# Which weights are asked for first, and a new order for the whole program: linear attention followed by a gated mixer on one core

## The chip, the cores and the metric

The kernel runs on one core of one Trainium2 chip. The metric is device time in microseconds (us) for one launch, the median of several runs.

## The reference, cut to what matters

For each of 8 batches there are 8 heads of 576 tokens with 64 features. Everything is float32 in memory.

```python
kv  = einsum('bhsd,bhse->bhde', k, v)
out = einsum('bhsd,bhde->bhse', q, kv)
x   = out / sqrt(mean(out*out, -1) + 1e-6) * g_norm      # then (batch, 576, 512)
theta  = x @ w_theta                                      # 512 x 512
zr, zi = x * cos(theta), x * sin(theta)
y = einsum('ts,bsd->btd', w_tok_r, zr) + einsum('ts,bsd->btd', w_tok_i, zi)   # 576 x 576 each
u = x + y
return u + relu(u @ w_ch)                                 # 512 x 512
```

## The kernel before

One batch has 576 tokens: four tiles of 128 tokens (j = 0 to 3) and a tail of 64. The tail is packed so that it fills 128 partitions at half width, and what concerns it has an "e" in its name. Each batch passes through the same chain of tasks:

- `kv` (L244, 80 fp32 rows of the trace for each batch) multiplies keys by values into PSUM. `ko` (L260) copies the result to the block-diagonal `kbd`.
- `qt` and `qo` (L279, L287) turn the queries on TensorE for batches 0 to 2; later batches use a transposing DMA on SP's queue (`qd`, L294). `raw` (L305) is query times kbd.
- `sq` (ScalarE, L330), `ss` (VectorE, L340) and `rt` (GpSimd, L346; for batch 0 ScalarE and VectorE) make one over the root of the head's mean square. `x` (VectorE, L368) scales by it.
- `xt` and `xc` (L391, L412) turn x on TensorE and copy it out, times g, to `xT`; from batch 4 on a DMA does the turning (`xd`, `xo`).
- `th` (L448) is x times theta's weights `wth`. `pt`, `ar`, `ab`, `si`, `co` (L453 to L487) bring the angle into range, take its absolute value and give sine and cosine. `z` (L493) multiplies them by x.
- `y` (L522) mixes the tokens, in three parts of three matmuls each for every one of 8 output pieces, with the turned token weights `wT`. `um` (L537) makes u.
- `ut`, `uo` (L544, L557) or, for batches 3 to 6, the DMA `ud` turn u back. `v` (L568) is u times the channel weights, `fin` (L573) adds and clips, `st` (L609) stores.

The token weights come in two halves, `w_tok_r` and `w_tok_i`. Each is turned on TensorE once, in nine pieces (`wt`, L622): even pieces and the tail need the i half and its 64 tail rows, odd pieces and the tail the r half.

All of these are 1189 tasks in a list. Each task has an engine, or two between which one is chosen, and the tasks whose results it needs. The table `TURNS` (L32) says in which order they are issued: a plain number is a task on its first engine, a number with a star is the same task on its second engine, and `r9` or `a5` are so many idle matmuls on TensorE, which keep it running and compute nothing that is used. `play` (L86) issues them in that order. Nothing is moved afterwards, so each engine and each DMA queue meets its instructions in the order of the table.

The loads around the change stand on three queues. SP carries batch 0's keys and tails and then all later keys and values; ACT carries batch 0's values; POOL (GpSimd) carries the queries and all weights, since these change from float32 to float16 on the way. Three small GpSimd instructions hold transfers back on purpose. `hold p` (L231) reads one number of batch 0's v tails and so waits until they have landed; whatever comes behind it on POOL's queue waits too. `hold w` (L228) reads a number of theta's weights, and batch 1's v (`load v1`, on SP, with batch 1's k behind it) waits for it. `hold v` waits for batch 1's v and stands ahead of the queries of batches 1 and 2 and the channel weights `wch`.

Of the kernel before, what the change touches and what calls it, by code (L numbers as in the profile page):

```python
# [33 lines left out]
58* 31 32 36 37 38 33* 34 39* 40* 73 43 74* 50* 44 45 59 75 51 65 25 60 12 61 76 46 66 77 47 62 63  # L34
52 r9 48 64 67 53 68 84 82 85 99 54 78 83* 69 70 100 135 139 136 140 79 80 71 55 56 72 92 90 91* 93
86 87* 127 88 101 89* 94 106 120 81 103 102 128* 95 131 137 113 132* 96 138* 104 121 122 105 129 97
114 107 130* 98 108 115 109 143 133 124 123* 134 169 173 141 161 210 211 212 213 110 125 111 144 117
116* 118 142 126 112 119 174 162 216 217* 214 215 170 230 163 223 218 219 231* 165 175 232 171 164
354 203 205 204 206 220 172 176 388 233 221 234 389 166 145 157 167 153 237 224 374 146 154 222 168
225 238* 235 226 236 155 156 227 147 149 244 239 158 375 245 240 251 150 151 187 159 252 241 228 242  # L40
261 253 262 188* 152 148 160 229 381 189 263 243 246 254 382 194 367 255 268 190 368* 256* 177 178*
275 257 182 247 265 264* 266 269 248 249 361 362 363 364 276 270 277 278 267 258* 250 183 279 271*
282 184 259 272 273 283 192 365* 366* 369 383 284 185 260 289 197 199 370 358 209 208 359 360 509
356 357 355 191 529 518 512 513 514 515 371 372 384 193 290 198 274 291 385 195 280 285* 373 281 200
386 292* 293 286 516 294 179 376 387 324 312 404 390 325 377 517 196 540 505 506 507 508 287 180 405
378 316 317 313 402 391 295 288 419 395 314 318 326 392 379 393 380 403 420 396 315 319 327 394 304
397 300 398 399 412 421 400 413 414 519 305 520 401 521 522 408 406 407 320 306 307 296 530 410 531
416 415 422* 423 424 417 411 301 409* 532 533 297 321 302 303 523 308 309 322 323 310 524 525 311
418 534 298 426 427 343 433 548 434 299 428 526 541 542 543 440 441 442 443* 435 544 186 511 527 430
429* 652 653 654 655 658 669 645 646 647 181* 510 425 549* 431 444 656 437 657 344* 545 345 546 554  # L50
563 436 432 555* 346 547* 528 564 445 565 348 584 349 535 536 438 328 556 338 467 468 475 659 585
557 446 439 537 586 339 469 470 558 476 477 455 340 451 452 588 660 329 661 649 785 651 538 650 539
787 662 341 456 670 453 454 560 559* 567 587* 671 672 663 561 457 550 447 552 471 472 458 553 478
673 674 347 680 648 686 473 474 675 333 335 334 336 794 337 805 783 330 676 677 331 577 664 463 589
566* 551 578 568 562 448 449 450 579 464 465 459 665 570 666 678 667 580* 581 571 569 572 466 582
460 461 574 687 668 573* 575 462 679 788 789 790 791 350 681 499 501 351 583 500 682 792 793 502 590
576 688 784 683 684 201* 921 479 699 700 692 693 694 795 489 490 591 685 701 332 503* 342 202 816
781 690 796 797 798 703 611 612 592 494 607 613 614 608 593 594 609 491 806 689* 713 702* 696 807
695* 697 492 808 610 595 619 620 621 481 495 484 596 597 698 799 809 714 715 810 623 782 822 493 930
704 480 482 800 598 622 599 600 811 706 801 802 707 812 705 708 710 709* 691* 615 616 603 604 605  # L60
813 485* 606 803 804 496 617 618 601 486 716* 717 602 786 814 639 817 720 641 487 818 640 819 497
642 924 925 926 927 820 815 821 823 721 722 723 711 718 712 719 928 929* 835 836 483 626 624 625 498
488 824 633 630 634 837 931 828 631 724 932 725 726 747 627 748 755 838* 628 749 936 750 756 727 829
937 938 830 933 743 744 745 757 758 746 735 728 729 730 636 632* 952 917 352* 826 941 919 918 939
934 504* 644* 825 849 751 637 739 740 940 741 947 832 839 831* 833 850 834 759 752 753 851 935 948
949 731 942 736 732 733 950 638* 754 742 842 737 853 840 852* 943 827 843 734 944 777 856 775 854
776 857 920 635 629 1059 951 738 953 760 762 761 945 1053 1054 1055 1056 844 841 946 858 845* 954
846 859* 955 855 778 847 860 956 957 848 1057 861 1058 922 958 1070 862 769 772 763 1060 863 864 770
773 1061 1062 865 959* 866 879 880 881 766 1065 1066 764 882 867 868 964 971 1063 1064 1071 1067 923
771 774* 960 962 1068 767 965 966 869 887 883 884 888 972 973 1069 885 871 1072 1073 765 643 353 895  # L70
1081 768* 1074 779* 974 870 886 967* 975 968 963 976 977 889 890 1075 872 992 1076 875 873 876 961
1077 993 874 994 877 891 892 893 969 996 995* 997 1078 878 978 979 894 970 985 980 986 982 981* 911
1082 913 912* 987 988* 983 914 998 984 908 899 905 1015 1016 989 990 896 780 897 898 1087 900 901
1079 991 999 1000 1017 1001 906 1018 1080 902 1011 1012 1013 903 1002 1083 1088 909 1014 1084 1093
1094 1095 1100 1101 1007 1008 1009 1019 1023 1102 1027 1028 1029 1024 1089 1085 916 1031 904 1086
1096* 1090 1097 1104 907 1091 910 1030 1103* 1025 1003 1004 1005 1020 1021 1010 1026 1006 1107 1022
1105 1098 1092 1106 1099 1108 1114 1115 1109 1121 1110 1047 1034 1033 1049 1048 1050 1116 1038 1041
1111 1122 1123 1112 1113 1124* 1125 1118 1126 1117* 1119 1032 1039 1040 1042 1043* 1156 1035 1036
1144 1157 1148 1149 1145 1152 1153 1127 1120 1146 1150 1154 1158 1151 1147 1155 1159 1037 1044 1136
1132 1045 1180 1178 1137 1138 1139 1179 1181 1133 1128 1183 1185 1173 1140 1141 1134 1184 1186 1129  # L80
1130 1135 1182 1188 1187 1131 1142 1143 1175 1160 1162 1046* 1174* 1176 1161* 1177 915* 1165 1163
1164 1051* 1167 1170 1052* 1166 1168 1171 1169 1172
""".split()


# [14 lines left out]
def kernel(  # L100
# [61 lines left out]
    wth = const.tile([P, NKC, C], FP16, name="wth")  # L162
# [17 lines left out]
    def tails_of(t):  # L180
        return t[:, H * NJ * D:H * NT * D].rearrange("p (h e) -> p h e", h=H)
# [29 lines left out]
    def token_in(w_in, at):  # L211
        nc.gpsimd.dma_start(
            out=wn[at][:], in_=w_in[0:SM, :].rearrange("(p j) s -> p j s", j=NJ)
        )

    def token_tail_in(w_in, at):
        nc.gpsimd.dma_start(out=wnt[at][:], in_=w_in[SM:S, :])
# [13 lines left out]
    def hold_pool(src):  # L231
        nc.gpsimd.tensor_copy(out=gate[:], in_=src)
# [422 lines left out]
    got, q_got, k_got = {}, {}, {}  # L655
# [9 lines left out]
    for hp in range(NHP):  # L665
# [265 lines left out]
```

## Time and profile before

| what | value |
|---|---|
| time, three runs | 207.13, 207.51 and 210.13 us; the median is 207.51 |
| the profiled execution | 206.56 us, of which the instructions span 204.6 |
| granted TensorE clock | 1.0 in every stretch |
| moved by DMA | 43.14 MB; 33.06 read, 9.44 written in HBM |

The profile is that of one execution. Busy times count an engine's own work; the time of a matmul includes its way through the array, so several overlap. "L534" is a line of the kernel. In a list of instructions the first column is the start, the second the time taken, both in us; the brackets at the end tell how long the engine was idle before it and what ended that. In the table of stretches "(x52)" is a number of instructions. In the DMA rows q0 is POOL's queue, q1 SP's and q10 ACT's.

### The profile page before, as it was taken

What the parts mean: (1) busy time and instruction counts of PE and PEld (TensorE: products, weight loads), DVE (VectorE), ACT (ScalarE), POOL (GpSimd) and SP (SyncE); (2) the same over time, 40 slices, a digit from 0 to 9 for tenths busy, and PEclk for the clock granted to TensorE, in tenths of its full rate; (3) what the DMA queues carried; (4) which work ended last, traced back from release to release, by engine and by line L of the source; (5) the groups of instructions that cost most, each with busy time, mean ns of one, the idle gap of its engine ahead of it and who ended that gap; (6) DMA issues with size and microseconds to landing.
All of it is one profiled execution on the core that took longest, in us unless ns stands there. A gap on an engine that the chain in (4) does not pass through costs nothing.

```text
span 204.6 us, 5267 instructions
## 1 busy us (share of the span) xinstructions
PE 188.3 (92%) x2078; PEld 132.8 (65%) x2078; DVE 172.5 (84%) x362; ACT 137.6 (67%) x272; POOL 86.4 (42%) x92
## 2 busy tenths in 40 slices
PE   0299899999999999999999999998989999999992
PEld 0275568885786777676776767665856746755671
DVE  6029896789999999999898999897989999689473
ACT  2006899748799587987896769576945983976101
POOL 8022061263965564874609382283629430101210
PEclk9999999999999999999999999999999999999999
DMA  6999999999999999999999999799988652853154
GB/s 196 271 197 193 294 268 193 275 354 236 254 187 193 277 264 260 310 221 137 199 226 248 237 221 180 170 283 305 287 187 194 150 103 70 189 129 135 35 154 154
DMA packets 74951, 43.14 MB, mean 211 GB/s; under 512 B 44576, under 2 KB 71008, under 8 KB 74928
## 3 DMA queue, kind: packets, MB, share of 16 engines
q1 hardware_dynamic: 58688, 32.12, 66.9%
q0 software_dynamic: 15040, 9.52, 29.9%
q10 hardware_dynamic: 1200, 1.18, 1.7%
q8 instruction: 16, 0.26, 0.5%
q14 instruction: 7, 0.06, 0.1%
HBM read 33.06 MB, written 9.44 MB: 208 GB/s over the span
## 4 chain that ended last, share of the span: by engine, by line
PE 67%; ACT 12%; DVE 8%; DMA 7%; issue 2%; POOL 1%; DVEq 0%; ACTq 0%; POOLq 0%
PE y L534 29%; PE th L440 11%; PE v L440 11%; DMA vt<-in_v_dram 5%; PE kv L255 3%; PE raw L312 3%; DMA uD<-wn 2%; DVE arg L463 2%; ACT kbd L275 2%; ACT sc L488 2%; PE wps L630 2%; ACT sc L481 1%; ACT arg L471 1%; ACT xT L408 1%; PE qps L270 1%
## 5 line engine op out<-in xcount | busy, mean ns | idle before, releaser
L353 POOL TENSOR_TENSOR rt<-ss,mhalf 128x8 f32<-128x8 f32 (+1 forms) x35 | 54.6, 1563 | 65.7 <-DVE ss L343 65.5
L534 PE MATMUL y<-wT,zm 128*128 128x320 f16 (+1 forms) x512 | 76.8, 286 | 0.7 <-DVE ot L576 0.5
L534 PEld LDWEIGHTS <-zm 128*128 128x128 f16 x512 | 48.0, 98 | 15.8 <-issue 1.2
L539 DVE SCALAR_TENSOR_TENSOR wn<-y,gcol,xT 128x320 f16<-128x320 f32 (+1 forms) x64 | 31.0, 511 | 6.7 <-PE y L534 6.3
L440 PE MATMUL th<-wth,xT 128*128 128x512 f16 x128 | 32.1, 380 | 0.9 <-ACT xT L408 0.6
L456 ACT ACTIVATE arg<-th 128x512 int32<-128x512 f32 (+1 forms) x40 | 21.8, 554 | 14.1 <-PE th L440 13.7
L440 PE MATMUL v<-wch,wn 128*128 128x512 f16 x124 | 30.7, 380 | 0.0
L255 PE MATMUL kv<-vt,kt 128*64 128x64 f32 x640 | 21.9, 230 | 9.3 <-DMA vt<-in_v_dram 9.3
L334 ACT ACTIVATE sqb<-raw 128x512 f32<-128x512 f32 x32 | 18.9, 595 | 14.4 <-PE raw L312 14.3
L255 PEld LDWEIGHTS kv<-vt,kt 128*64 128x64 f32 x640 | 20.9, 144 | 10.2 <-issue 9.7
L488 ACT ACTIVATE sc<-arg,quarter 128x512 f16<-128x512 f32 (+1 forms) x40 | 26.6, 675 | 0.3
L463 DVE SCALAR_TENSOR_TENSOR arg<-th,arg 128x512 f32<-128x512 f32 (+1 forms) x40 | 25.0, 632 | 1.9 <-ACT arg L456 1.5
L481 ACT ACTIVATE sc<-arg 128x512 f16<-128x512 f32 (+1 forms) x40 | 22.7, 582 | 3.2 <-DVE arg L463 2.8
L343 DVE TENSOR_REDUCE ss<-sqb 128x8 f32<-128x520 f32 x32 | 22.0, 687 | 2.4 <-ACT sqb L334 2.4
L511 DVE TENSOR_TENSOR zm<-x,sc 128x1024 f16<-128x1024 f16 x32 | 21.8, 686 | 1.8 <-ACT sc L488 1.5
L375 DVE TENSOR_TENSOR x<-raw,rt 128x512 f16<-128x512 f32 x32 | 21.8, 685 | 0.8 <-POOL rt L353 0.5
L440 PEld LDWEIGHTS <-xT 128*128 128x128 f16 x128 | 11.6, 98 | 11.1 <-ACT xT L408 1.0
L440 PEld LDWEIGHTS <-wn 128*128 128x128 f16 x124 | 11.5, 98 | 10.7 <-issue 0.4
L471 ACT ACTIVATE arg<-arg 128x512 f32<-128x512 f32 (+1 forms) x31 | 17.5, 575 | 1.2 <-DVE arg L463 1.1
L534 PE MATMUL y<-wT,zt 128*128 128x320 f16 (+1 forms) x64 | 18.3, 286 | 0.0
L275 ACT CAST kbd<-kv 64x256 f16<-64x256 f32 (+1 forms) x24 | 8.5, 356 | 13.5 <-PE kv L255 13.2
L275 ACT COPY us<-ups 128x512 f16<-128x512 f16 (+1 forms) x17 | 8.5, 498 | 12.6 <-PE ups L270 11.5
(83 smaller groups left out, 229.3 us busy)
## 6 DMA issues: line engine op xcount, KB each, us to landing
vt<-in_v_dram SPq DMA_DIRECT2D x7, 1024.0 KB, 9.8
kt<-in_k_dram SPq DMA_DIRECT2D x7, 1024.0 KB, 7.9
out_dram<-ot SPq DMA_DIRECT2D x24, 256.0 KB, 2.8
qh<-in_q_dram POOLq DMA_DIRECT2D x7, 512.0 KB, 8.6
out_dram<-ot POOLq DMA_DIRECT2D x7, 256.0 KB, 4.0
kt<-in_k_dram SPq DMA_DIRECT2D x2, 512.0 KB, 4.6
vt<-in_v_dram ACTq DMA_DIRECT2D x2, 512.0 KB, 9.0
kt<-in_k_dram SPq DMA_DIRECT2D x8, 128.0 KB, 7.9
```

The source lines that it names most:

```text
L255: nc.tensor.matmul(t[i * D:(i + 1) * D, hp - lo, :], ks, vs, start=(hp == lo and j == 0), stop=(hp == lo + n - 1 and j == NT - 1),)
L343: nc.vector.reduce_sum(out=ss[:], in_=sq_sb.pop((b, j))[:], axis=AXX)
L353: nc.gpsimd.tensor_tensor(out=rt[:], in0=ss[:], in1=mhalf[:, 0:h], op=ALU.pow)
L375: nc.vector.tensor_tensor(out=x_pair[b, p][:, :, a * HC:(a + 1) * HC].rearrange("p t (h e) -> p h t e", e=D), in0=r[:].rearrange("p (h t e ...
L440: nc.tensor.matmul(t[:], piece(kc), w[:, kc, :], start=first, stop=last)
L456: nc.scalar.activation(out=arg[:, 1, :].bitcast(I32), in_=th_ps[b, j][:], func=AFT.Copy, scale=1.0 / TURN)
L463: nc.vector.scalar_tensor_tensor(out=arg[:, 0, :], in0=th_ps.pop((b, j))[:], scalar=1.0 / TURN, in1=arg[:, 1, :].bitcast(I32), op0=ALU.mul ...
L481: nc.scalar.activation(out=sc[:, 0, :], in_=arg_sb[b, j][:, 0, :], func=AFT.Sin, bias=0.0, scale=TURN * SHRINK,)
L488: nc.scalar.activation(out=sc_sb[b, j][:, 1, :], in_=arg_sb.pop((b, j))[:, 1, :], func=AFT.Sin, bias=quarter[:], scale=-TURN * SHRINK,)
L511: nc.vector.tensor_tensor(out=dst, in0=x.unsqueeze(1).broadcast_to((P, 2, w)), in1=sc[:], op=ALU.mult)
L534: nc.tensor.matmul(t[:, 0:hi - lo], s, wT[:, w, lo:hi], start=n == 0, stop=n == len(z) - 1)
L539: nc.vector.scalar_tensor_tensor(out=uTb[b % NUT][:, c, lo:hi], in0=y_ps.pop((b, h, c))[:, 0:hi - lo], scalar=gcol[:, 0:1], in1=xTb[b % NX ...
```

## The change

The weights of theta and the i half of the token weights change places at `hold p`: the main part of the i half (`load toki`) is issued ahead of it, and theta's weights (`load wth`) depend on it now. The r half depends on it as before. The tail rows of the i half (`load tokie`) lose the dependence on `hold p`, but the new table issues them behind `load wth`. Batch 1's v still waits for theta's weights, through `hold w`.

`TURNS` is new throughout. The same 1189 tasks are issued in another order, other copies and absolute values have the star, and there are 7 idle matmuls (`a1`, `a1`, `a5`) where there were 10 (`r1`, `r9`).

```diff
 TURNS = """
-3 4 0 1 2 5 6 7 9 8 11 10 13 29 30 41 r1 49 35 14 15 16 17 18 19 22 23 20 21 24 26 207 28 27 42* 57
...
+0 1 6 7 8 3 4 41 9 13 a1 49 42* 50 5 11 2 10 29 30 31 32 15 16 14 17 18 19 22 24 26 27 207 28 25 20
...
-    got["wth"] = [add("load wth", "POOL", theta_in)]
+    got["tok", 0] = [add("load toki", "POOL", lambda: token_in(moe_w_tok_i, 1)),
+                     add("load tokie", "POOL", lambda: token_tail_in(moe_w_tok_i, 1))]
     hold = add("hold p", "POOL", lambda: hold_pool(tails_of(vt[0])[0:1, 0, 0:1]), [v0[2]])
-    got["tok", 0] = [add("load toki", "POOL", lambda: token_in(moe_w_tok_i, 1), [hold]),
-                     add("load tokie", "POOL", lambda: token_tail_in(moe_w_tok_i, 1), [hold])]
+    got["wth"] = [add("load wth", "POOL", theta_in, [hold])]
     got["tok", 1] = [add("load tokr", "POOL", lambda: token_in(moe_w_tok_r, 0), [hold]),
                      add("load tokre", "POOL", lambda: token_tail_in(moe_w_tok_r, 0), [hold])]
```

The first place is the start of POOL's queue, as the difference shows it. `wn` and `wnt` are the token weights and their tail rows, `gate<-vt_66` is `hold p`.

```order
 L206 DMA qe_71<-in_q_dram 64x4x64 x2
+L212 DMA wn_86<-in_moe_w_tok_i_dram 128x2304
+L232 COPY gate<-vt_66 1x1
 L220 DMA wth<-in_moe_w_theta_dram 128x4x512
-L232 COPY gate<-vt_66 1x1
-L212 DMA wn_86<-in_moe_w_tok_i_dram 128x2304
 L217 DMA wnt_88<-in_moe_w_tok_i_dram 64x576
 L212 DMA wn_85<-in_moe_w_tok_r_dram 128x2304
```

The i half's main part now stands ahead of the gate and theta's weights behind it; the i half's tail rows come behind theta's weights, and the r half is where it was.

The second place is the start of SP's queue. `kt_64` and `vt_66` are batch 0's keys and values, the 64x8x64 rows their tails; `vt_67` and `kt_65` are batch 1's.

```order
 L184 DMA kt_64<-in_k_dram 128x4x256 x2
+L190 DMA vt_66<-in_v_dram 64x8x64
+L226 DMA gcol<-in_g_norm_dram 64x1
 L190 DMA kt_64<-in_k_dram 64x8x64
-L190 DMA vt_66<-in_v_dram 64x8x64
-L226 DMA gcol<-in_g_norm_dram 64x1 x2
+L226 DMA gcol<-in_g_norm_dram 64x1
 L184 DMA vt_67<-in_v_dram 128x8x256
-L190 DMA vt_67<-in_v_dram 64x8x64
 L184 DMA kt_65<-in_k_dram 128x8x256
 L190 DMA kt_65<-in_k_dram 64x8x64
+L190 DMA vt_67<-in_v_dram 64x8x64
```

Batch 0's v tails, which `hold p` waits for, are asked for ahead of its k tails, and batch 1's v tails come last of its four loads instead of second.

The third place is ScalarE's queue around the sines of batch 1, before the change:

```order
L481 ACTIVATE sc<-arg 128x512
L471 ACTIVATE arg<-arg 128x512
L488 ACTIVATE sc<-arg,quarter 128x512
L456 ACTIVATE arg<-th 128x512 x2
L275 COPY us<-ups 128x512
L481 ACTIVATE sc<-arg 128x512
L471 ACTIVATE arg<-arg 128x512
```

and the same place in the changed kernel:

```order
L481 ACTIVATE sc<-arg 128x512
L456 ACTIVATE arg<-th 128x512
L488 ACTIVATE sc<-arg,quarter 128x512
L408 ACTIVATE xT_83<-xps,gcol 128x4x128
L456 ACTIVATE arg<-th 128x512
L481 ACTIVATE sc<-arg 128x512
L488 ACTIVATE sc<-arg,quarter 128x512
```

The absolute values (L471) of these tiles are gone from ScalarE; they stand on VectorE now (L473), as does the copy of u. Over the whole program these moves go from ScalarE to VectorE: 8 absolute values of full tiles and 2 of tails, 2 copies of u and 3 of its tails, 3 tails of `xT` and 1 piece of the token weights. From VectorE to ScalarE go 2 copies of turned queries, 1 copy of kbd and 2 of batch 0's, 1 of `xT` and 1 of its tails. Of the stores, 25 are on POOL's queue where there were 16.

More of the change, by code (lines that the diff above doesn't have):

```diff
@@ L79 @@
[L79 to L82, printed above, removed]
+0 1 6 7 8 3 4 41 9 13 a1 49 42* 50 5 11 2 10 29 30 31 32 15 16 14 17 18 19 22 24 26 27 207 28 25 20
+21 23 35 36 37 38 39* 33 34 43 44 40 73 57 58* 59 65 45 46 74* 47 60 75 61 76 66 62 a1 a5 51 52 48
@@ new lines @@
+375 235 168 222 225 226 236 227 237 381 145 238 146 147 382* 239 240 251 158 159 187 228 148 241
+188* 160 189 190 242 252 253 244 245 261 254 192 151 262 229 243 246 268 193 156 247 263 248 249 255
+256 367 194 368* 152 257 275 182 361 362 363 364 264 195 265 269 270 250 271 266 267 183* 258 276
+277 272 278 259 282 184 273 365 260 366* 369 383 283 279 370 274 185 289 197 199 384 280 290 371
+198* 284 286 285* 287 200 385 281 291 293 512 513 514 515 358 209 208 509 359 510 372 505 529 518
+386 360 373 288 387 179 177 376 312 324 292* 294 178 180 377 516 404 405* 313 395 325 517 390 378
@@ new lines @@
+1107 1106 1092* 1099 1108 1114 1121 1047 1049 1115 1109 1110 1048 1050 1116 1111 1122 1112 1123 1033
+1113 1032 1041 1038 1035 1156 1157 1042 1036 1039 1117* 1118 1125 1124* 1119 1126 1120 901 916*
+1043* 1040* 1037 1052 503* 1051 1148 1144 1149 1145 1152 1153 1127 1158 1159 1154 1155 1150 1146
+1132 1147 1151 1044 1045 1183 1185 1184 1186 1128 1178 1180 1179* 1181 1140 1133 1141 1134 1135 1173
+1129 1142 1130 1136 1143 1137 1131 1138 1139 1175 1174* 1176 1160 1162 1161* 1163 1177 1164 1165
+1167 1188* 1046* 1182* 504* 1187* 1166* 1168 1169 1170 1171 1172
```

81 lines of the change are left out of this document (36 added, 45 removed).

## The prediction

> **What bounds the kernel now.** I read the totals and the chain that ended last first, then the table of stretches, then the start instruction by instruction.
>
> ```profile
> span 204.6 us, 5267 instructions
> PE 188.3 (92%) x2078; PEld 132.8 (65%) x2078; DVE 172.5 (84%) x362; ACT 137.6 (67%) x272; POOL 86.4 (42%) x92
> PE 67%; ACT 12%; DVE 8%; DMA 7%; issue 2%; POOL 1%; DVEq 0%; ACTq 0%; POOLq 0%
> ```
>
> TensorE (PE) holds two thirds of the chain, and VectorE (DVE) is busy almost as long as PE. Which of them limits depends on the stretch. I cut the span where PE begins, where the key-value product (kv) of batch 1 begins (32.8), where that of batch 7 begins (144.7), and look at one inner stretch by itself. Columns: length, then busy time of PE, weight loads, DVE, ScalarE (ACT) and GpSimd (POOL), clock, DMA share, GB/s.
>
> ```profile
> 9.10:32.80 23.70, 22.25 (x235) 14.86 (x235) 18.08 (x46) 14.63 (x33) 6.50 (x12) 1.00 1.19 235
> 32.80:144.70 111.90, 110.32 (x1359) 81.02 (x1359) 102.31 (x205) 88.03 (x173) 59.84 (x52) 1.00 1.16 240
> 52.00:107.00 55.00, 54.31 (x738) 40.08 (x737) 52.27 (x106) 47.12 (x97) 32.75 (x29) 1.00 1.18 229
> 144.70:201.00 56.30, 55.72 (x498) 36.88 (x492) 48.06 (x98) 33.42 (x65) 15.61 (x17) 1.00 0.62 143
> ```
>
> Between 32.8 and 144.7 DVE works 102.31 of 111.9 us (91.4%), and from 52 to 107 it works 52.27 of 55 (95.0%). That is the highest share it holds for long. PE shows as busy throughout, but busy is not full pace, so I priced its work by its densest pieces on the chain (start, length, what):
>
> ```profile
> 32.86 2.48 PE kv L255 x80
> ...
> 70.53 0.45 PE xps L270 x8
> ...
> 163.70 1.73 PE th L440 x8
> ...
> 165.79 0.44 PE v L443 x8
> ...
> 174.84 5.63 PE y L534 x45
> ```
>
> A y matmul is 5.63/45 = 0.125 us, a full theta or channel matmul 1.73/8 = 0.216, a tail one 0.055, a kv row 0.031, a 128-wide turn or raw 0.056. With the counts: 576 x 0.125 = 72; 252 x 0.216 = 54.5; 128 x 0.055 = 7; 640 x 0.031 = 20; 318 x 0.056 = 18; the narrow ones, the token weights' turns and 10 idle matmuls about 10.5. Together 182 us. Ahead of batch 1's kv stand 17.7 of them, in 23.7 us, so 6.0 are lost at the start. Behind it stand 164.3, and from 32.8 to 201 are 168.2, so only some 4 us are lost there, 2.4 of them before 144.7. **PE therefore leaves little to gain after 32.8 us; DVE is close behind it in the middle; the start has the largest loss.**
>
> The start, from the timeline:
>
> ```profile
> 4.38 0.80 POOL L220 DMA_DIRECT2D wth<-in_moe_w_theta_dram  x1
> ...
> 13.93 0.17 POOL L232 COPY gate<-vt 1x1 f32<-1x1 f32 x1 [8.74 <-DMA vt<-in_v_dram]
> 14.05 0.55 POOL L212 DMA_DIRECT2D wn<-in_moe_w_tok_i_dram  x1
> ...
> 17.02 0.18 POOL L229 TENSOR_TENSOR gate<-vt,wth 1x1 f32<-1x1 f32 x1 [0.78 <-DVE qT L277]
> 17.22 0.37 SPq L184 DMA_DIRECT2D vt<-in_v_dram  x1
> ...
> 17.79 2.11 PE L640 MATMUL idle<-fill,ident 128*128 128x512 f16 x9
> ...
> 19.90 5.71 SPq L190 DMA_DIRECT2D kt<-in_k_dram  x1
> ...
> 20.80 0.68 ACT L408 ACTIVATE xT<-xps,gcol 128x512 f16<-128x512 f16 x1
> ...
> 21.53 1.04 PE L440 MATMUL th<-wth,xT 128*128 128x512 f16 x4 [0.60 <-ACT xT L408]
> ```
>
> The first theta matmul (21.53) waits for xT, not for its weights. Those had landed by 17.02, when `hold w` ran and let batch 1's v go (17.22). The idle matmuls at 17.79 fill a hole; the last thing before theta is batch 0's own chain raw, squares, root, x, xT.
>
> **The change part by part.** *Theta behind `hold p`.* What each queue moved, from the DMA view of 14.5 to 17, of 17 to 21 and of 24.4 to 27, and the times to landing:
>
> ```profile
> q0 software_dynamic: 311, 0.47, 118.1%
> ```
>
> ```profile
> q0 software_dynamic: 251, 0.79, 103.9%
> q1 hardware_dynamic: 1, 0.00, 0.1%
> ```
>
> ```profile
> q1 hardware_dynamic: 1209, 0.81, 113.7%
> ```
>
> ```profile
> wn<-in_moe_w_tok_i_dram POOLq DMA_DIRECT2D x1, 576.0 KB, 6.5
> wn<-in_moe_w_tok_r_dram POOLq DMA_DIRECT2D x1, 576.0 KB, 8.5
> wth<-in_moe_w_theta_dram POOLq DMA_DIRECT2D x1, 512.0 KB, 12.5
> ```
>
> POOL's queue (q0) alone fills the engines from 14.5 to 21, at 0.47/2.5 to 0.79/4 = 0.19 to 0.20 MB a us. Before, theta landed at 4.38 + 12.5 = 16.9 and the i half at 14.05 + 6.5 = 20.5. Swapped, the i half, 0.06 MB more, lands at about 17.2, and theta 0.5/0.2 = 2.6 us later, at 19.8. It is issued when `hold p` lets go, at 13.9 or earlier (v's tails now stand second on SP), so it queues behind the i half in any case, and how early the gate opens is worth nothing. Theta at 19.8 is 1.7 us ahead of 21.5: the first theta matmul does not feel it. The i half at 17.2 is 3.3 us earlier, so one turn of it now fits ahead of the second x turn and theta, where PE waited. That turn also reads the i half's tail rows, which stand behind theta: about 20.2, just in time. I take 0.3 us of gain here.
>
> *Batch 1's v behind theta.* It goes out at about 20.1, 2.9 later. Behind it on SP's queue are batch 1's k, k tails and v tails, and kv of batch 1 waits for all four. But v, issued at 17.22, moved one packet before 21, because the engines were full of weights. With v later the weights have them alone and end earlier. v and k (2.3 MB) then run at 0.81/2.6 = 0.31 MB a us, 7.4 us from about 23.6, to 31. Before, the last of them landed at 19.90 + 11.3 = 31.2:
>
> ```profile
> kt<-in_k_dram SPq DMA_DIRECT2D x1, 128.0 KB, 11.3
> ```
>
> Batch 1's kv begins at 32.86, so this is hidden with 1.7 us to spare, and I cost it at nothing. Without that cover the 2.9 us delay costs 2.9 - 1.7 = 1.2; that is the upper end of the start, and -1.5 (a quarter of the 6.0 lost there) the lower. *Fewer idle matmuls*, 3 x 0.216 = 0.65, stand in the hole and belong to those 1.5.
>
> One rule of the Trainium skill speaks against the swap ("DMA: Bandwidth & Descriptors", section on queues, rings and completion order): each DMA engine takes turns between the queues that have work, packet by packet, so a load issued early gets its share beside another queue. By that rule v would lose its turn for 2.9 us, at most 1.5 us of full rate, which is inside the 1.7 us to spare. The trace agrees only from 21 on; from 17.22 to 21 v has one packet beside 251 of q0.
>
> *The new order from batch 1 on.* PE does the same work there. DVE and ACT do not: a count of the two tables gives the moves, and these rows their prices (count, then busy, mean ns):
>
> ```profile
> L471 ACT ACTIVATE arg<-arg 128x512 f32<-128x512 f32 x24 | 14.7, 621 | 0.6 <-DVE arg L463 0.6
> L473 DVE TENSOR_SCALAR arg<-arg 128x512 int32<-128x512 int32 x8 | 3.6, 452 | 0.1
> L277 DVE COPY us<-ups 128x512 f16<-128x512 f16 x6 | 2.5, 419 | 0.5 <-PE ups L270 0.5
> L277 DVE COPY us<-ups 128x256 f16<-128x256 f16 x1 | 0.3, 281 | 0.0
> L277 DVE COPY qT<-qps 128x512 f16<-128x512 f16 x7 | 3.0, 422 | 9.4 <-PE qps L270 9.4
> L277 DVE CAST kbd<-kv 64x256 f16<-64x256 f32 x6 | 2.5, 420 | 0.1
> L277 DVE CAST kbd<-kv 64x128 f16<-64x128 f32 x6 | 1.7, 288 | 0.2
> L410 DVE TENSOR_SCALAR xT<-xps,gcol 128x512 f16<-128x512 f16 x8 | 3.8, 478 | 0.0
> L275 ACT COPY us<-ups 128x512 f16<-128x512 f16 x10 | 5.9, 587 | 11.5 <-PE ups L270 11.5
> ```
>
> To DVE come 8 x 0.452 (absolute values), 2 x 0.29 (their tails, priced like the 0.281 copy), 2 x 0.419 + 6 x 0.281 (u, its tails, xT's tails) and one weight piece of about 0.45: 7.2 us. Away go 2 x 0.422, 2 x 0.420, 4 x 0.288, 0.478 and about 0.35: 3.7. DVE gains 3.5 us of durations, and ACT loses about 6, 8 x 0.621 being most of it.
>
> Adding mean durations in table order between batch 1's and batch 7's kv gives DVE 114.0 us in the old table and 119.8 in the new, because the new one also places DVE work earlier. The old 114.0 showed as 102.31 busy (neighbours overlap), a factor of 0.897; the new ones come to 107.5 us. To fit in 111.9 DVE would have to run at 96.1%. At its best long share, 95.0%, the stretch takes 113.2: +1.3. At its old share, 91.4%, it takes 117.6: +5.7. The best that PE allows is its 2.4 us of loss: -2.4. I take +1.3, since ACT, relieved by about 4 us in the same stretch (101.3 to 97.2 counted likewise), should make DVE wait less than before.
>
> *The end.* Behind 144.7 PE has the same tasks in both tables, and DVE about 1 us less. The last copy of u, 0.587 us on ACT before, is one of 0.419 on DVE: -0.2, with bounds of -1.5 (PE's loss there) and +0.5 (a store on POOL that ends last).
>
> **Sum:** -0.3 + 1.3 - 0.2 = +0.8 on the profiled execution's 206.56, its span of 204.6 and 2 us around it, so 207.4. The median shown is 207.51, 0.95 above the profiled one, which makes the forecast **208.3 us**: no change that can be told, since about 2% (4 us) is what this kernel's measurement can tell.
>
> **The rivals.** *DVE becomes the bound.* It keeps its old share of waits between 32.8 and 144.7, so its 5.2 us of added busy time push batch 7's kv by 5.7: 206.56 - 0.3 + 5.7 - 0.2 + 0.95 = 212.7, slower. It decides from batch 2's kv on, at the absolute values. For it: DVE's 95% from 52 to 107 hold there already. Against it: ACT, with 12% of the chain, has less to do. Chance 0.2. A rule of the skill sharpens it ("SBUF — State Buffer", section on the shared port): DVE in its two-port modes and GpSimd lock each other out, and the absolute values and copies are candidates for such modes. The roots on GpSimd show a spread that would fit:
>
> ```profile
> L353 POOL TENSOR_TENSOR rt<-ss,mhalf x35: 1006/1642/1959, 39.4 to 174.7; 128x8 f32<-128x8 f32 x28, 128x4 f32<-128x4 f32 x7
> ```
>
> No run here shows which instruction stretched them.
>
> *ACT was the brake.* Its chain pieces shrink, DVE runs above 95%, and PE gets back all it loses: -2.4 in the middle, -0.8 at the start, -0.2 at the end, 206.56 - 3.4 + 0.95 = 204.1; with the whole of the bounds (-1.5 - 2.4 - 1.5) 202.1. For it: 12% of the chain on ACT. Against it: DVE has to reach 96%. Chance 0.25.
>
> *Batch 1's kv waits for its loads.* v's first packet comes as long after its issue as before and the weights are no faster: k lands at 34.1, kv of batch 1 begins 1.2 later, and the rest follows: 208.3 + 0.3 + 1.2 = 209.8. Chance 0.1. Here the change would not do what it says on the one side that can lose: the swap brings only a wait, and the order carries the rest.
>
> **How the numbers follow.** My forecast, a result between 206.5 and 210, has 0.45, DVE 0.2, ACT 0.25, the loads 0.1. The range of 204.0 to 213.0 holds the forecast, the loads, the centre of the DVE case and that of the ACT case; 0.2 stay outside, most of it in the ACT case's lower half. Faster by over 2% (below 203.4) is 0.17, a good half of the ACT case and a little of the start's bound; slower by over 2% (above 211.7) 0.22, the DVE case and the two mishaps that add to it; 0.61 for within 2%.
>
> **What would show it.** Right: theta lands at 19 to 20.5 and its first matmul begins within 0.5 us of 21.5; batch 1's v is issued near 20 and its kv begins within 1 us of 32.8; batch 7's kv begins 0 to 3 us after 144.7 with DVE at 94 to 96% between them; PE's stretch behind it stays at 56 us. Wrong: PE waiting for theta's weights or the i half's tail rows, kv of batch 1 waiting for a load, DVE below 92% with PE idle on it, or batch 7's kv ahead of 143.

## The result, and the profile after

| | before | after |
|---|---|---|
| median of 20 runs each (us) | 207.12 | 210.75 |
| lowest and highest (us) | 206.04, 210.13 | 208.41, 212.96 |
| the profiled execution (us) | 206.56 | 208.41 |

The change costs time: the ratio is 1.015, with a 95% interval of 1.012 to 1.018. It leaves out runs that lie over 1.5% above the fastest of the same kernel; where a kernel's runs spread widely, its median over all runs is given beside it. The forecast was 208.3, so the time came out 2.45 above it, inside the range of 204 to 213 and inside the 2% that I had called "no change". The profiled execution of the changed kernel is the lowest of its 20 runs, so its trace shows the least of the loss.

The totals of the changed kernel, then its stretches, cut at the same events as before (PE begins, kv of batch 1 begins, kv of batch 7 begins), with the one between batch 5's and batch 6's kv besides:

```profile
span 206.6 us, 5255 instructions
PE 187.0 (91%) x2075; PEld 133.3 (65%) x2075; DVE 173.7 (84%) x371; ACT 132.9 (64%) x263; POOL 90.9 (44%) x101
```

```profile
10.70:33.41 22.71, 21.11 (x230) 15.06 (x230) 16.22 (x40) 16.43 (x38) 6.71 (x12) 1.00 1.21 234
33.41:147.25 113.84, 110.48 (x1358) 81.08 (x1359) 103.83 (x214) 83.20 (x165) 62.14 (x55) 1.00 1.22 240
100.83:126.14 25.31, 22.69 (x273) 16.49 (x274) 21.05 (x44) 17.87 (x35) 12.69 (x13) 1.00 1.23 229
147.25:203.00 55.75, 55.44 (x492) 37.14 (x488) 49.48 (x104) 31.80 (x61) 17.80 (x23) 1.00 0.55 134
```

The stretch between batch 5's and batch 6's kv, in the kernel before:

```profile
100.72:123.35 22.63, 22.51 (x274) 16.45 (x274) 21.27 (x43) 17.79 (x36) 11.81 (x10) 1.00 1.14 223
```

The spans differ by 2.0 us. Batch 1's kv begins 0.6 late (33.41 against 32.8). By batch 5's kv this is nearly regained (100.83 against 100.72). Then one stretch takes 25.31 us where it took 22.63: 2.7 us lost in one place, with the same PE work, 22.69 busy against 22.51. Behind batch 7's kv nothing is lost. So the loss is a hole, not a general slowing. **The hole**, from the timeline of the changed kernel:

```profile
85.55 1.01 SPq L184 DMA_DIRECT2D vt<-in_v_dram  x1
...
94.08 2.02 SPq L298 DMA_TRANSPOSE qD<-qh  x1
...
96.19 0.62 SPq L190 DMA_DIRECT2D vt<-in_v_dram  x1
...
97.30 4.96 SPq L421 DMA_TRANSPOSE xD<-x  x1
...
108.06 1.15 ACT L408 ACTIVATE xT<-xD,gcol 128x1024 f16<-128x1024 f16 x1 [2.81 <-DMA xD<-x]
...
109.27 1.04 PE L440 MATMUL th<-wth,xT 128*128 128x512 f16 x4 [2.50 <-ACT xT L408]
```

and what the DMA view says of the transpose issued at 97.30 (count, then us from issue to landing):

```profile
xD<-x SPq DMA_TRANSPOSE x1, 10.7
```

Batch 4's x is turned by a DMA on SP's queue (`xd 4 0`). It stands there behind the 1 MB of batch 6's values (85.55), a turn of batch 5's queries (94.08) and the 128 KB of batch 6's value tails (96.19), and takes 10.7 us to land. ScalarE stands idle for 2.81 us on it, and since it meets its instructions in the order of the table, all that it would do next waits too; PE then waits 2.50 for the `xT` that ScalarE makes. Before, the same transpose was ahead of that load:

```profile
95.27 1.25 SPq L421 DMA_TRANSPOSE xD<-x  x1
...
99.97 0.57 SPq L184 DMA_DIRECT2D vt<-in_v_dram  x1
...
102.22 1.13 ACT L408 ACTIVATE xT<-xD,gcol 128x1024 f16<-128x1024 f16 x1
```

```profile
xD<-x SPq DMA_TRANSPOSE x1, 3.2
```

It landed in 3.2 us, 3.7 before ScalarE came to it. The Trainium skill says of such queues ("DMA: Bandwidth & Descriptors", section on queues, rings and completion order) that on each DMA engine the descriptors of one ring are consumed in ring order; the trace agrees: by the DMA view the four take 14.5, 10.5, 8.9 and 10.7 us, so they land at 100.1, 104.6, 105.1 and 108.0, in the order in which they were issued, and the transpose behind the bulk takes three times as long as before.

**The start** of the changed kernel, from the timeline:

```profile
11.60 0.75 POOL L220 DMA_DIRECT2D wth<-in_moe_w_theta_dram  x1
...
12.09 4.54 PE L255 MATMUL kv<-vt,kt 128*64 128x64 f32 x80
...
16.56 0.40 PE L312 MATMUL raw<-kbd,qT 128*128 128x128 f16 x4
...
19.26 0.18 POOL L229 TENSOR_TENSOR gate<-vt,wth 1x1 f32<-1x1 f32 x1 [5.27 <-DMA wth<-in_moe_w_theta_dram]
19.47 0.39 SPq L184 DMA_DIRECT2D vt<-in_v_dram  x1
...
22.08 0.69 ACT L408 ACTIVATE xT<-xps,gcol 128x512 f16<-128x512 f16 x1
...
23.04 1.03 PE L440 MATMUL th<-wth,xT 128*128 128x512 f16 x4
```

Theta's weights are there at 19.26, but the first theta matmul begins at 23.04, 1.5 later than before. It isn't the weights: the chain ahead of it is late from batch 0's kv on. PE now begins with a turn of queries, at 10.70, where it began with kv at 9.11. Batch 0's kv stands behind that turn as one block of 80 rows that takes 4.54 us, 57 ns a row. Before, its last 32 rows took 36 ns each, and the first raw began 0.86 earlier:

```profile
14.21 1.15 PE L255 MATMUL kv<-vt,kt 128*64 128x64 f32 x32
...
15.70 1.30 PE L312 MATMUL raw<-kbd,qT 128*128 128x128 f16 x8
```

From the first raw to batch 1's kv the changed kernel takes 16.85 us (16.56 to 33.41), and the kernel before 17.09 (15.70 to 32.79). So the start loses all that it loses ahead of the first raw.

### The profile page after: what moved, and what is told of

It reads as the page before. It is cut to its first block, busy times and chain, and to the rows that moved or that the text cites. A ratio compares the mean times of both kernels' runs of the same rounds, so it can differ in the third digit from the quotient of the medians.

```text
span 206.6 us, 5255 instructions
## 1 busy us (share of the span) xinstructions
PE 187.0 (91%) x2075; PEld 133.3 (65%) x2075; DVE 173.7 (84%) x371; ACT 132.9 (64%) x263; POOL 90.9 (44%) x101
## 5 line engine op out<-in xcount | busy, mean ns | idle before, releaser
L534 PE MATMUL y<-wT,zm 128*128 128x256 f16 (+1 forms) x512 | 76.7, 286 | 0.2
L539 DVE SCALAR_TENSOR_TENSOR wn<-y,gcol,xT 128x256 f16<-128x256 f32 (+1 forms) x64 | 31.5, 512 | 3.9 <-PE y L534 3.7
L334 ACT ACTIVATE sqb<-raw 128x512 f32<-128x512 f32 x32 | 18.4, 597 | 13.1 <-PE raw L312 13.0
L255 PEld LDWEIGHTS kv<-vt,kt 128*64 128x64 f32 x640 | 21.5, 149 | 0.8 <-issue 0.5
L440 PEld LDWEIGHTS <-xT 128*128 128x128 f16 x128 | 11.5, 98 | 12.1 <-ACT xT L408 2.7
L534 PE MATMUL y<-wT,zt 128*128 128x256 f16 (+1 forms) x64 | 18.3, 286 | 0.0
L270 PE MATMUL qps<-ident,qh 128*128 128x128 f16 x48 | 4.8, 234 | 10.7 <-DMA qh<-in_q_dram 10.7
L576 DVE SCALAR_TENSOR_TENSOR ot<-v,us 128x512 f32<-128x512 f32 (+1 forms) x23 | 13.6, 593 | 0.8 <-PE v L440 0.4
L613 POOL DMA_DIRECT2D out_dram<-ot x12 | 6.9, 578 | 16.8 <-DVE ot L576 16.8
```

The lines of the kernel that those rows point to most:

```text
L255: nc.tensor.matmul(t[i * D:(i + 1) * D, hp - lo, :], ks, vs, start=(hp == lo and j == 0), stop=(hp == lo + n - 1 and j == NT - 1),)
L440: nc.tensor.matmul(t[:], piece(kc), w[:, kc, :], start=first, stop=last)
L534: nc.tensor.matmul(t[:, 0:hi - lo], s, wT[:, w, lo:hi], start=n == 0, stop=n == len(z) - 1)
L539: nc.vector.scalar_tensor_tensor(out=uTb[b % NUT][:, c, lo:hi], in0=y_ps.pop((b, h, c))[:, 0:hi - lo], scalar=gcol[:, 0:1], in1=xTb[b % NX ...
```

## The experiments

Twelve kernels. Theory A is that the order loses its time where x's transposes stand behind bulk loads on SP's queue; theory B, the prediction's, that VectorE's added work is felt; the others are told in the expectations where they come up. In the lines of four kernels (the swap alone, the order alone, `xd 4 0` first, and the changed kernel with idle matmuls) the line numbers are 10 higher than elsewhere. The diffs of orders show SP's queue by task names, with the stores left out: `load v6` and `load k6` are batch 6's values and keys (1 MB each), `v6e` and `k6e` their tails, `qd 5 0` a turn of batch 5's queries, `xd 4 0` and `xd 4 1` the turns of batch 4's x.

### The two parts of the change, each alone

The swap alone: the order before, with `load toki` ahead of `hold p` and `load wth` behind it.

> The kernel before with the swap of the weights alone, its own order otherwise: the i half ahead of the hold, then the hold, theta's weights, the i half's tail rows, the r half. Theory A and the prediction: theta lands near 19.5 and nobody waits, so the time is within 0.7 us of before. Theory C (the swap itself costs, by theta or by batch 1's v arriving late): 1.5 us or more above before, with batch 1's kv that much later.

Measured: 207.89 against 207.47, ratio 1.0028 (0.9996 to 1.0059): no difference that can be told. Its start, from the timeline:

```profile
20.42 0.18 POOL L239 TENSOR_TENSOR gate<-vt,wth 1x1 f32<-1x1 f32 x1 [4.42 <-DMA wth<-in_moe_w_theta_dram]
...
21.18 1.04 PE L450 MATMUL th<-wth,xT 128*128 128x512 f16 x4 [0.60 <-ACT xT L418]
```

Theta's weights are there just 0.8 us ahead of the first theta matmul, which still waits for xT alone, and batch 1's kv begins at 32.43. So theta's weights land in time, as the prediction has it. One wait is there that nobody expected: kv of batch 2 waits 1.5 us in all for its values in this trace (0.51 and 1.00), where before it does not.

The order alone: the changed kernel with the dependences of the kernel before, and `load wth` back at its old place.

> The changed kernel's order with the swap undone: theta first, then the hold, then the i half. Theory A: as the changed kernel, within 0.7 us, so 2.5 to 3.5 above before. Theory C: 1.5 us or more below the changed kernel.

Measured: 211.44 against 207.47, ratio 1.0157 (1.0100 to 1.0215). **The order carries the whole loss.** The profiled execution here took 212.68 us, one of the longer runs. Its longest wait of PE at theta, and its stretches around it (the column behind POOL is the granted clock):

```profile
PE th L450 <- ACT xT L418: 4.2, 1, 4.2
```

```profile
108.00:110.00 2.00, 0.00 (x0) 0.00 (x0) 0.00 (x0) 0.48 (x1) 0.00 (x0) 1.00 0.89 209
110.00:112.00 2.00, 1.28 (x4) 0.46 (x5) 0.85 (x3) 1.98 (x5) 0.39 (x1) 0.52 1.09 355
112.00:114.00 2.00, 2.00 (x10) 0.88 (x9) 1.94 (x6) 1.68 (x3) 2.00 (x4) 0.63 1.19 309
114.00:116.00 2.00, 2.00 (x21) 1.35 (x19) 1.22 (x4) 0.85 (x2) 1.29 (x2) 1.00 1.40 324
```

The same hole as in the changed kernel, but 4.2 us deep, and with a second price: just behind it the granted clock is down to one half for some 3.4 us (0.52, 0.63, then 1.00). That takes (1 - 0.52) x 2 + (1 - 0.63) x 2 = 1.7 us of full pace besides. The Trainium skill has this as the activity clock gate ("TensorE: Matmul & The Clock Gate", Part 1): idle TensorE falls to half rate, in steps of about 3.4 us. The trace agrees on the step.

### Where the order loses it

The changed kernel, with `xd 4 0` ahead of the bulk:

```diff
 load k5e
-load v6
-qd 5 0
-load v6e
 xd 4 0
+qd 5 0
+load v6
+load v6e
 qd 5 1
 load k6
 xd 4 1
```

> The changed kernel with one edit in its table: batch 4's x is sent to its turning DMA ahead of the turning of batch 5's q and of batch 6's v and v tails, which follow it on SP's queue. Theory A (the loss sits where this DMA lands 10.7 us after its issue, behind the bulk load, and ScalarE waits 2.8 and TensorE 2.5 us for it): the DMA lands within 4 us, both waits are gone, the time falls by 2 to 2.7 us against the changed kernel. Theory B (VectorE has too much to do, the prediction's rival): the waits move, the time stays within 0.7 us of the changed kernel.

Measured: median 211.04 of 12 runs (207.2 to 213.82), ratio 1.0052 (1.0004 to 1.01), which rests on its three lowest runs. The wait at `xd 4 0` is gone, it lands in 3.3 us. In its place, from the timeline:

```profile
114.81 1.15 ACT L418 ACTIVATE xT<-xD,gcol 128x1024 f16<-128x1024 f16 x1 [2.85 <-DMA xD<-x]
```

`xd 4 1`, now behind batch 6's values and keys, is late instead (8.8 us). PE waits only 0.5 us for it in this trace, which is the lowest run. That run is 1.2 us below the lowest of the changed kernel, but the median is no lower. By the letter of the expectation this is theory B's outcome, waits that move and a time within 0.7 us; that VectorE is not the reason is shown only by later kernels. What it shows is that the place was right for this one wait, and that the stall moves on.

All of batch 6's loads moved back behind `xd 4 0` and `qd 5 1`, where they stood before (only `load k6` is still ahead of `qde 5 2`, which it was behind):

```diff
 load k5e
-load v6
-qd 5 0
-load v6e
 xd 4 0
+qd 5 0
 qd 5 1
-load k6
+load v6
 xd 4 1
+load v6e
+load k6
 qd 6 0
```

> The changed kernel with batch 6's bulk loads behind x's transposes of batch 4 on SP's queue, as in the order before: xd 4 0 first, then qd 5 0, qd 5 1, load v6, xd 4 1, load v6e and load k6. Theory A (the order loses its time because xd 4 0 and xd 4 1 stand behind bulk loads): both land within 5 us of their issue, ACT's and PE's waits there are below 1 us, and the median falls from the change's 210.75 to 207.5 to 208.7, since the longer runs with a PE stall there go with it. Theory B (VectorE's added work is the loss): VectorE has the same work, so 210 to 211.5. Theory C (any move of loads only shifts the stall to the next transpose, as when only xd 4 0 was moved): 210 to 211 with a new wait of 2 us or more on SP's queue between batch 4 and batch 6.

Measured: 210.81 against 207.07, ratio 1.0173 (1.0135 to 1.0211). Theory A falls in this form, and C is right. `xd 4 0` and `xd 4 1` land in 3.8 and 5.7 us with no wait on them. The stall is at batch 4's third transpose (`xde 4 2`), from the timeline:

```profile
123.83 0.28 DVE L410 TENSOR_SCALAR xT<-xD,gcol 128x256 f16<-128x256 f16 x1 [3.81 <-DMA xD<-x]
...
124.63 0.42 PE L553 MATMUL ups<-ident,wn 128*64 128x128 f16 x3 [2.83 <-DVE wn L539]
```

```profile
124.00:131.00 7.00, 6.11 (x105) 5.88 (x106) 6.57 (x15) 2.99 (x7) 4.41 (x5) 0.53 1.22 226
```

VectorE stands 3.8 us, PE 2.8, and the clock falls to one half for nearly 7 us, (1 - 0.53) x 7 = 3.3 us of full pace.

The same move in the other kernel: before, with the bulk ahead of the transposes.

```diff
 load v5
+load v6
 qde 4 2
 load v5e
+qd 5 0
+load v6e
 xd 4 0
-qd 5 0
 qd 5 1
-load v6
 xd 4 1
-load v6e
 qde 5 2
```

> The kernel before with nothing changed but SP's queue around 86 to 97 us: load v6 ahead of qde 4 2, and qd 5 0 and load v6e ahead of xd 4 0, as in the changed kernel. Theory A: xd 4 0 takes 8 us or more from issue to landing instead of 3.2, ACT and then PE wait 2 to 4 us, and the median is 1.5 to 3.5 us above the kernel before (ratio 1.007 to 1.017), with a mean clock of about 0.992 in many runs. Theory B: VectorE's work is that of before, so within 0.7 us of it.

Measured: 211.27 over 12 runs in two groups, four at 207.7 to 208.4 and eight at 210.5 to 212.3; ratio 1.0069 (1.0028 to 1.011), which rests on the four and the lowest of the eight. A loss appears, as A has it, but not the waits of 2 to 4 us. The profiled execution is the lowest one, and shows a small wait:

```profile
103.15 1.15 ACT L408 ACTIVATE xT<-xD,gcol 128x1024 f16<-128x1024 f16 x1 [0.87 <-DMA xD<-x]
```

The number I had given missed: this transpose took 4.3 us to land, not 8, and it was the issue that came 3.5 us later (98.81), since `qd 5 0` ahead of it waited for its queries. By then the 1 MB, issued at 84.06, had landed (12.2 us, at 96.3); in the changed kernel it lands 2.8 us behind the issue of the transpose. The mean clock stayed at 0.997 or above in all these runs, so the upper group isn't explained by the clock; none of it has a trace, and where it loses 3.7 us against the lower one (by the medians) stays open. So the place on SP's queue costs the kernel before something, but this run does not show that it costs it at this transpose.

If the stall only moves, the question is room: are the DMAs asked for too much in this stretch? The next kernel is the changed one with seven eighths of batch 6's keys and values not read.

```diff
-                       lambda t=t, src=src: heads_in(nc.sync, t, src, b, all8),
+                       lambda t=t, src=src: heads_in(nc.sync, t, src, b, slice(0, 1) if b == 6 else all8),
```

> The changed kernel, with one head of eight loaded of batch 6's main keys and values (the other seven heads keep what the buffers held, so batch 6's output is not the reference's): 1.75 MB less of reads around 85 to 113 us, all instructions and the order as in the changed kernel. Theory E (the new order leaves the transposing DMAs too little room beside the bulk loads in that stretch, wherever exactly the loads stand): x's transposes of batch 4 land within 5 us, TensorE's gap between batch 5's and batch 6's kv is below 0.5 us, the clock stays above 0.997, batch 7's kv begins before 145.5, and the median is 207.0 to 208.5. Theory F (the stall comes from the engines' own order, the DMAs are only what it shows up at): a gap of 2 us or more stays, 210 to 211.

The control is the same edit in the kernel before.

> The control: the kernel before, with the same seven heads of batch 6's keys and values left out (batch 6's output is not the reference's). Theory E: the kernel before had room enough, so within 0.7 us of it. If it gains more than 1 us, the kernel before was slowed by these loads too, and what the lighter changed kernel gains is not the order's loss alone.

Measured: the changed kernel falls from 210.75 to **206.44** (ratio to before 0.9949, 0.9919 to 0.9978), the kernel before stays at 207.39 (1.0011, 0.9986 to 1.0037). Here is 84 to 126 in the kernel before, in the changed one, in the light changed one and in the light one of before (the last number is GB/s):

```profile
84.00:126.00 42.00, 41.63 (x488) 30.27 (x486) 39.27 (x79) 34.77 (x69) 23.55 (x20) 1.00 1.19 220
```

```profile
84.00:126.00 42.00, 39.38 (x415) 27.81 (x415) 37.24 (x78) 29.93 (x58) 23.04 (x23) 1.00 1.25 233
```

```profile
84.00:126.00 42.00, 42.00 (x499) 30.41 (x498) 39.98 (x85) 30.97 (x61) 25.44 (x25) 1.00 1.10 200
```

```profile
84.00:126.00 42.00, 41.64 (x490) 30.25 (x488) 39.31 (x79) 34.77 (x69) 24.03 (x21) 1.00 1.04 184
```

The changed kernel moves 233 x 42 = 9.8 MB here, the one before 220 x 42 = 9.2. With 1.75 MB less asked for, PE has no hole in this stretch (42.00 of 42), and the order is not slower than before. So the loss needs batch 6's loads: it goes when they go, while the kernel before does not gain by the same edit. With the traces that have the hole, in which PE's wait goes back to a transposing DMA each time, this puts the loss on transposes that come late beside bulk loads. One wait of this kind is left behind the stretch: PE stands 1.6 us at 130, where VectorE waits for a turn of u by DMA. One detail missed: the third transpose still took 7.5 us, above the 5 expected, but was covered, as one of 8.0 us is in the kernel before.

Is it the nine more stores on GpSimd's queue? The changed kernel, with every store on its old queue (`st` and `ste` with the star of the table before):

> The changed kernel, with every store on the queue that it had in the kernel before (16 on GpSimd's queue instead of 25), order as in the changed kernel. In the profile GpSimd's queue's packets take 6.8 us of all 16 engines more than before and SP's 1.0 less. If the stores on GpSimd's queue are what crowds the transposing DMAs: the gap at batch 4's theta below 1 us and 207.5 to 209. If it is the bulk loads and the order of SP's queue: within 0.8 us of the changed kernel's 210.75, gap 2 us or more.

Measured: 210.7 against 207.09, ratio 1.0119 (1.0076 to 1.0161): no gain that can be told, so the stores are not what the time is lost by. But the gap at theta, which I had expected to stay at 2 us, was absent from its trace: `xd 4 0` lands in 7.9 us instead of 10.7, and ScalarE waits 0.6 for it. PE's longest wait is one of 1.5 us at 130, where VectorE waits for a turn of u by DMA. The stretch from 84 to 126 in this trace:

```profile
84.00:126.00 42.00, 41.74 (x480) 29.98 (x480) 39.57 (x83) 31.56 (x61) 22.12 (x20) 1.00 1.25 249
```

The DMAs move more here than in the changed kernel (249 against 233 GB/s), and PE has hardly a hole. So the rate by itself does not tell whether a transpose comes late. Two stores of 256 KB that the changed kernel issues on GpSimd's queue at 95.25, and this one on SP's behind `xd 4 0`, may be a part of the hole's depth in its trace; these runs don't show it.

### Is VectorE's added work felt?

The run with the bulk late, and the absolute values on the engines that had them before:

> The run with the bulk loads late, and besides that the absolute values on the engines that had them before (eight full ones and two tails back from VectorE to ScalarE, one other way), all else in the new order. Theory B (VectorE's added 3.5 us are felt between batch 1's and batch 7's kv, the term of +1.3 in the prediction): 1 us or more below the run with the bulk loads late, batch 7's kv earlier by as much. Theory A: within 0.7 us of it, either way, since VectorE had slack there; ScalarE's added 5 us may cost up to 1.

Measured: 211.85 against 210.81 without the move; no gain. The stretch from batch 1's to batch 7's kv in this kernel, and in the light changed kernel, which has the new engines:

```profile
32.79:147.85 115.06, 110.87 (x1359) 81.34 (x1360) 102.31 (x207) 86.60 (x172) 62.02 (x55) 1.00 1.19 239
```

```profile
33.06:145.33 112.27, 110.31 (x1358) 81.10 (x1359) 103.96 (x215) 83.28 (x165) 62.14 (x55) 1.00 1.15 229
```

With VectorE back at the 102.31 us of before the stretch takes 115.06; with VectorE at 103.96 and batch 6's loads light it takes 112.27. That is 0.4 more than before, and 0.6 less than in the light kernel before, the control (112.89, with VectorE at 102.41). Theory B falls: by these traces VectorE's added work costs no more than that 0.4.

### The start

The changed kernel, with 28 idle matmuls ahead of everything on PE (`a28` in front of the table):

> The changed kernel with 28 idle matmuls more, at the very front of TensorE's queue, before any data has landed. Theory D (the start is late because TensorE takes up work only at 10.7 and then runs batch 0's 80 kv rows at half pace, 107 ns a pair against 58 before in its second block): the pairs run at 58 ns, batch 0's first raw moves from 16.6 to about 15, the first theta from 23.0 to 21.5, batch 1's kv by 0.6 to 1.2, and the time falls by 0.5 to 1.2 us. If pace at the start is not what counts: batch 1's kv stays at 33.4 within 0.3.

Measured: 210.61, ratio to before 1.0141 (1.0096 to 1.0186), so the 0.5 to 1.2 us did not come. Batch 1's kv does begin at 32.24, 1.2 earlier, but batch 2's kv is then ahead of its loads:

```profile
53.42 1.79 PE L265 MATMUL kv<-vt,kt 128*64 128x64 f32 x54 [0.99 <-DMA kt<-in_k_dram]
```

The early start is not the only cause of such a wait: batch 2's kv waits 1.5 us in the trace of the swap alone too, 0.5 in that of the order alone and 0.4 in that with the stores as before. The hole ahead of batch 6's kv is there as well: 25.06 us from batch 5's kv.

Both edits together, bulk late and 28 idle matmuls:

> The run with the bulk loads late, and 28 idle matmuls at the front of TensorE's queue, so that batch 0's kv runs at full clock. If the start's loss is the half clock: batch 1's kv at 32.2 to 32.5 instead of 33.4, and if nothing behind takes it back, 0.5 to 1.2 us below the run with the bulk loads late. If kv of batch 2 waits for its loads as in the earlier warm run, the gain is given back there and the time is within 0.5 us of the run with the bulk loads late.

Measured: 209.79, ratio 1.0136 (1.0110 to 1.0163), 1.0 below the run with the bulk late alone, though the two intervals overlap. Batch 1's kv is at 32.06; batch 2's waits 1.5 us for its keys here as well, which I had expected to take the gain back. Its stall at batch 4's third transpose is 2.2 us, and the clock falls behind it for 3.4.

The kernel before, with 24 idle matmuls in front:

> The kernel before with 24 idle matmuls at the front of TensorE's queue, so that batch 0's kv runs at full clock from its first row. If the half clock at the start is what the start loses: batch 1's kv 0.5 to 1.2 us earlier than 32.8, and 0.3 to 1 us off the median. If kv of batch 2 then waits for its loads, as in the changed kernel with idle matmuls in front: batch 3's kv at 58.4 or later and the median within 0.4 us of the kernel before.

Measured: **205.88 against 207.09, ratio 0.9941 (0.9912 to 0.9969)**: faster than both kernels, and the best of the complete ones. From its timeline:

```profile
1.46 7.95 PE L640 MATMUL idle<-fill,ident 128*128 128x512 f16 x24 [1.46 <-DVE fill L892]
9.33 1.15 PE L255 MATMUL kv<-vt,kt 128*64 128x64 f32 x32
```

The first 32 rows of kv take 1.15 us where they took 1.97 in the kernel before. Batch 1's kv begins at 32.33, 0.46 earlier, just under the 0.5 I had set, and the median falls by 1.2, more than the 1 I had set; batch 2's kv doesn't wait. At batch 7's kv (143.16) the profiled execution is 1.5 ahead, because a wait of 0.9 us at 138.8, for an x of VectorE's, is gone too. Whether that second part comes from the earlier start or from the spread between runs, one trace doesn't tell.

## Why the prediction was right in its range and wrong in its cause

- **The swap: right about the waits, its gain by luck.** Theta's weights were put at 19.8 and landed at 11.60 + 7.5 = 19.1 in the changed kernel and by 20.4 in the swap alone; batch 1's v was put at 20.1 and went out at 19.47 and 20.63; no kv of batch 1 waited for a load. The swap alone brought batch 1's kv 0.36 forward in its trace where I had -0.3, but not by the swap: its first raw is already 0.36 earlier (15.34 against 15.70), and from there to batch 1's kv both take 17.09. What there is of a gain behind the first raw is the new order's: 16.85 in the changed kernel, and 16.87 in the order alone, which does not have the swap.
- **The start, -0.3: wrong by 0.9 in this trace.** My sign for a right prediction was the first theta matmul within 0.5 of 21.5; it came at 23.04. The step that failed is the working of the start, which looked at weights and gates and not at what PE does ahead of the first raw: batch 0's kv is now one block behind the queries' turns, and it runs while PE is still at half pace (57 ns a row against 36). How long it does differs from run to run. In the traces of the seven kernels that begin in the new order without idle matmuls in front, the block takes 3.40 to 4.61 us and batch 1's kv begins at 32.57 to 33.50, always 16.85 to 16.92 us behind the first raw. So the +0.6 of the changed kernel's trace (4.54 us for the block) is near the upper end of what this order gives.
- **The middle, +1.3: nearly the size of one trace, not the cause.** It measured 113.84 - 111.90 = +1.9. The prices of the moved work were right, as the groups of the changed kernel show:

```profile
L473 DVE TENSOR_SCALAR arg<-arg 128x512 int32<-128x512 int32 x16 | 6.5, 420 | 0.1
L471 ACT ACTIVATE arg<-arg 128x512 f32<-128x512 f32 x16 | 10.0, 628 | 1.3 <-DVE arg L463 1.3
```

  16 x 0.420 where there were 8 x 0.452. Summed over all rows of the groups, count times mean, VectorE gains 2.9 us (191.7 to 194.6) where I had 3.5, and ScalarE loses 5.8 where I had 6. But "the new ones come to 107.5 us" failed: VectorE was busy 103.83, 91.2% of the stretch, below the 92% that was one half of a sign of being wrong; the other half, PE idle on VectorE, is not what the trace shows. Of the work that the table's order had placed in the middle, a part showed elsewhere: VectorE is busy 1.9 less at the start (18.08 to 16.22), 1.5 more in the middle, and 1.4 more at the end (48.06 to 49.48), where I had 1 less. A count between two rows of the table isn't a count between two moments. From batch 1's to batch 5's kv the new order even took 0.5 less than the old (67.42 against 67.93). All of the loss lies in the next batch, at a transposing DMA. I had read SP's queue at the start and not in the middle. That +1.3 and +1.9 lie close together is luck.
- **The end, -0.2: right in sign**; it is -0.55 by the spans (59.35 against 59.9), and PE's stretch is 55.75. That VectorE would have less to do there was wrong.
- **From the profiled execution to the median, +0.95: too little, it is 2.34.** I had taken the spread of the kernel before. The changed kernel's wait is one on a transposing DMA, and its depth differs: 2.5 us in one trace, 4.2 with a clock drop in that of the order alone. The mean granted clock of every run tells more. Of the 20 runs of the changed kernel, 14 have 0.992 or less, and their median is 211.07; the other six, the profiled one among them, have 0.997 or more, and a median of 209.61. A mean of 0.992 over 209 us is 1.7 us of full pace, as much as the one drop in the trace of the order alone took. Of the 35 runs of the kernel before that were timed beside the last four kernels, 31 have 0.996 or more. So a drop of the clock goes with most of the 2.34; which wait sets it off in those runs, no trace shows.
- **The rivals.** "DVE becomes the bound" gave 212.7, nearest on the slow side, but two runs speak against its mechanism. "ACT was the brake" gave 204.1: ScalarE did lose 4.8 us of work in the stretch (88.03 to 83.20), and with batch 6's loads light the order is 0.65 below before and 0.95 below its control, so there may be something in it, at a fifth to a quarter of the 3.4 that I had put on it. The loads of batch 1 were not felt. The rival that was missing is the one that happened: the new order asks for bulk earlier on the queue that also turns x.

What stays open: which rows of the new order make the transposes late. With batch 6's loads back in their old places, `qd 6 0` still stood ahead of `xde 4 2` on SP's queue, which it doesn't in the order before; this wasn't tried by itself.

## What to carry to other kernels

When an order changes, read every DMA queue between the old and the new order, not the engines' rows alone, and for each transfer that an engine waits for ask which bulk now stands ahead of it and how much lead is left: in the changed kernel's trace 3.7 us of lead were used up where one load of 1 MB, its tails and one turn of queries now stand ahead. Moving one transfer out of the way told little here, since the stall moved on; taking away the traffic itself, in both kernels, showed that the loss goes with it. Idle matmuls from the first moment are worth trying where the first products are waited for: they took 1.2 us off the kernel before, and nothing that can be told off the changed one, where a wait for loads and the hole were still to come.

## What was not expected of the hardware

- PE's pace doubled 3.3 to 6.3 us after its first matmul, and the moment differs from run to run. In the kernel before PE began at 9.11 and the rows from about 14.2 on are the first quick ones; in the changed kernel it began at 10.70 and the quick rows come at 16.5; with the absolute values as before at 11.19 and 14.5; in the light kernel before at 8.69 and 15.0. The same 80 rows of kv took 4.54 us in the changed kernel and 3.53 in the trace of the order alone. The clock column of the stretches reads 1.00 there all the same, so the pace has to be read from the rows. The Trainium skill's figure for this ("TensorE: Matmul & The Clock Gate", Part 1) is about 3.4 us of sustained work, in a window that runs freely; the shortest time here agrees with it, the longest is nearly twice as long.
- A gap of PE of 2.2 us (bulk late with idle matmuls; a second of 0.4 follows 0.3 us later) or 2.8 (bulk late) was enough to halve the clock, for 3.4 and 6.8 us, while one of 2.5 in the changed kernel's profiled execution was not. The same section speaks of gaps over about 3.4 us; here the measurements decide, and they depend on more than the length.
- How much is moved does not tell how late a transpose lands. Between 84 and 126 the changed kernel moves 9.8 MB, and x's first two transposes of batch 4 land in 10.7 and 7.1 us; the kernel before moves 9.2, and they land in 3.2 and 4.7; with the stores as before it is 249 x 42 = 10.5 MB, and 7.9 and 7.7. In the trace of the order alone the first takes 12.1.
